# Gated mix of a state-space scan and a GELU layer: skip seeded into PSUM, gate as a weight column, B scale folded into C, shorter sine tables, halved weight strips

## The chip, the cores and the metric

The kernel runs on one core of one Trainium2 chip. The metric is device microseconds of one execution. A profile's span runs from the first to the last instruction; in these runs an execution is 1.8 to 2.1 us longer than its span. The granted TensorE clock of a run is its mean share of full speed; it was 0.99 to 1.00, and it is named where it matters.

Engines: PE is TensorE's matmul stream, PEld its weight loads, DVE is VectorE, ACT is ScalarE, POOL is GpSimd, SP issues most DMAs. A name with a q (SPq) is an engine's sequencer. PSUM is the memory into which TensorE writes; the program uses it as eight banks. An evacuation is the operation that reads a finished bank and so frees it. A hole is idle time of PE within a stage.

## The reference

One input x of 2048 x 640 goes through two branches, mixed by a gate per row:

```
g   = sigmoid(sum(x * gate_w))                       # per row
a   = 2 * Re(C @ h) + x * Dskip,  h_t = Lam_bar * h_(t-1) + B_bar @ x_t   # complex, 640 states
      with Lam_bar = exp(dt * Lam),  B_bar = ((Lam_bar - 1) / Lam) * (B_re + i B_im)
b   = gelu(x @ w1 + b1) @ w2 + b2                    # 640 -> 1728 -> 640
out = g * a + (1 - g) * b                            # bfloat16
```

## The kernel before

Rows are handled in 4 chunks of 512 (`CH`); the code counts them from 0, the text and the tables from 1. Per chunk PE does four stages: `ff1` (x·w1), `ssm` (B·x), `fin_b` (·w2) and `fin_a` (C·h). VectorE does the recurrence: it rotates B·x by a table of cosines and sines, so that the complex recurrence becomes two real scans, and rotates back. The rotation back carries the factor 2(Lam_bar - 1)/Lam in two tables of its own (OCOS, OSIN).

PE, VectorE and ScalarE execute in the order in which the program emits instructions. The author chooses VectorE's order at build time with an assumed clock: pending scan pieces are let out until the time at which an urgent operation is expected to be ready.

```python
    class Clock:
        pe = 6.5; act = 13.0; dve = 0.0
    def let_out(until):                      # emit pending scan pieces that would start before `until`
        while pend:
            ready, cost, fn = pend[0]
            start = max(ck.dve, ready)
            if start >= until: return
            pend.pop(0); fn(); ck.dve = start + cost
    def dve_now(ready, cost, fn):            # an urgent operation: after the pieces that fit before it
        let_out(ready); fn(); ck.dve = max(ck.dve, ready) + cost
    ...
    def ff1(c, group):                       # ff1(0, 7), later chunks ff1(c, 1)
        for g0 in range(0, KF, group):       # KF = 14 tiles of 128 columns of w1, the last of 64
            kfs = range(g0, min(KF, g0 + group))
            for kd in range(KD):             # KD = 5 strips of w1
                for kf in kfs:               # one PSUM bank per kf: `group` banks at once
                    if kd == 0: banks[kf] = bank()
                    ff1_mm(banks[kf], sizes[kf], c, kf, kd)
            ...                              # then the GELUs (ACT), from PSUM to SBUF
    ff1(0, 7)
    ...                                      # sine tables TCOS, TSIN, OCOS, OSIN, diag on VectorE
    ck.dve = 30.0                            # from here the scans are assumed to start
    ...
    def gates():                             # 80 matmuls with one column each
        for ti in range(NT):
            for kd in range(KD):
                nc.tensor.matmul(p[:, ti:ti + 1], lhsT=xT[c][:, kd, lo:lo + P], rhs=gw_c[:, kd:kd + 1], ...)
    def fin_a(c):
        for a in range(TPC):                 # 4 row tiles of 128
            for d0, d1 in cuts(ti):          # 384 + 256 columns
                p = bank()
                for j in range(2 * KS):
                    nc.tensor.matmul(p[:, 0:d1 - d0], lhsT=hs[c][:, j, lo:lo + P], rhs=CT[:, j % KS, d0:d1],
                                     start=(j == 0), stop=False)
                for o in range(d0, d1, P):   # skip term: x times a diagonal matrix
                    nc.tensor.matmul(p[:, o - d0:o - d0 + P], lhsT=xT[c][:, kd, lo:lo + P], rhs=diag[:, kd, :], ...)
                def f():                     # evacuation: ot = g * p + gb, frees the bank
                    nc.vector.scalar_tensor_tensor(out=ot[:, d0:d1], in0=p[:, 0:d1 - d0], scalar=gcol[:, 0, ti:ti + 1], ...)
                dve_now(ck.pe + 0.2, 0.5, f)
    ssm(0); ff1(1, 1); ssm(1); gates(); fin_b(0); fin_a(0)
    ssm(2); ff1(2, 1); fin_b(1); fin_a(1)
    ssm(3); ff1(3, 1); fin_b(2); fin_a(2); fin_b(3); fin_a(3)
```

## Time and profile before

The median was 235.54 us (235.34 to 235.76, four runs). The profiled run had a span of 234.1 us; the spans of other runs were mostly 233.0 to 233.9, so this profile is a slightly slow specimen.

Lines of the page of the kernel before follow: busy time of each engine with its share of the span and its instruction count; of part 2 the rows of PE and DVE over 40 equal slices (tenths busy); and of part 4 the chain of waits by engine.

```profile
PE 223.4 (95%) x1425; PEld 130.0 (56%) x1438; DVE 187.4 (80%) x429; ACT 87.6 (37%) x148; POOL 5.5 (2%) x16
...
PE   7978999999999999889999999999999999999994
...
DVE  1899999999999999999999999999999913300132
...
PE 65%; DVE 27%; issue 2%; ACT 2%; DMA 1%; ACTq 0%; DVEq 0%
```

PE is busy 95%, VectorE 80%, and the row of VectorE shows 9 from about 12 to 187 us: it has hardly a free moment there. The waits view of PE (who waited for whom; total us, times, longest):

```profile
PE bank L255 <- ACT gel L260: 2.4, 6, 1.4
PE bank L407 <- DVE ot L475: 2.2, 4, 0.9
```

The second line: B·x (L407) needs PSUM banks that the evacuation of C·h (ot, L475) has not yet freed. On PE's timeline (start, length, line, operation, idle before it and who ended it) the first line's hole looks like this:

```profile
15.71 0.38 PE L255 MATMUL bank<-xT_76,w_0_80 128*128 128x512 bf16 x1
17.49 0.38 PE L255 MATMUL bank<-xT_76,w_0_80 128*128 128x512 bf16 x1 [1.40 <-ACT gel L260]
18.07 0.38 PE L255 MATMUL bank<-xT_76,w_0_80 128*128 128x512 bf16 x1 [0.20 <-ACT gel L260]
...
27.63 0.39 PE L407 MATMUL bank<-xT_76,BT_re 128*128 128x512 bf16 x1
```

From 15.7 us PE gets one bank per GELU (0.58 us) instead of one per 0.216 us. ACT's timeline says why it began so late:

```profile
14.93 0.51 ACT L233 ACTIVATE hs<-gel,halfpi 128x256 f32<-128x256 f32 x1
15.45 1.28 ACT L260 ACT_TABLE_LOAD   x1
16.75 1.84 ACT L260 ACTIVATE gel<-bank,colB 128x512 bf16<-128x512 f32 x3
```

The gate matmuls and one cut of C·h on PE's timeline:

```profile
64.55 0.64 PE L422 MATMUL bank<-gw_c,xT_76 128*128 128x1 bf16 x20
...
66.56 1.62 PE L448 MATMUL bank<-w_sb,gel 128*128 128x384 bf16 x9
...
81.81 0.98 PE L465 MATMUL bank<-CT_re,hs 128*128 128x384 bf16 x5
82.62 0.98 PE L465 MATMUL bank<-CT_im,hs 128*128 128x384 bf16 x5
83.43 0.33 PE L470 MATMUL bank<-diag,xT_76 128*128 128x128 bf16 x3
83.60 0.71 PE L465 MATMUL bank<-CT_re,hs 128*128 128x256 bf16 x5
```

Three diagonal matmuls occupy PE from 83.43 to 83.60, although the groups view states 219 ns for one. Start-to-start is what counts, not stated durations: matmuls overlap. Last, VectorE's first scan piece, and the late evacuation of the first C tile, whose first cut PE had left at 83.60 us:

```profile
42.94 0.90 DVE L338 TENSOR_SCALAR diag<-ident,colB 128x128 bf16<-128x128 bf16 x5
43.76 0.68 DVE L347 TENSOR_TENSOR wa<-TCOS,bu 128x1024 bf16<-128x1024 bf16 x1
...
92.96 0.61 DVE L475 SCALAR_TENSOR_TENSOR ot<-bank,gcol,gb 128x384 bf16<-128x384 f32 x1
93.49 0.68 DVE L347 TENSOR_TENSOR wb<-TSIN,bu 128x1024 bf16<-128x1024 bf16 x1
94.09 0.48 DVE L475 SCALAR_TENSOR_TENSOR ot<-bank,gcol,gb 128x256 bf16<-128x256 f32 x1
```

### The profile page before, as it was taken

To read this page: it belongs to the slowest core of one execution; us is meant where nothing else is said; L and a number is where in the kernel's file an instruction comes from. 1 tells how busy PE (TensorE), PEld (TensorE's weight loads), DVE (VectorE), ACT (ScalarE), POOL (GpSimd) and SP (SyncE) were. 2 spreads that over 40 slices of the span, in tenths; PEclk is the share of its full clock that TensorE was granted. 3 is DMA by queue.
4 is the path that set the end of the run, shared out by engine and by line. 5 is a ranking of instruction groups with operands and counts; after the bars stand their busy time and mean duration, and the time that the engine had idled before them with its cause. 6 is when DMAs were issued, how large, how long until landed. Compare 5 with 4: busy or idle time off the path is not lost.

```text
span 234.1 us, 3628 instructions
## 1 busy us (share of the span) xinstructions
PE 223.4 (95%) x1425; PEld 130.0 (56%) x1438; DVE 187.4 (80%) x429; ACT 87.6 (37%) x148; POOL 5.5 (2%) x16
## 2 busy tenths in 40 slices
PE   7978999999999999889999999999999999999994
PEld 3532344444486777334446777644446767776672
DVE  1899999999999999999999999999999913300132
ACT  2885575655510500345662310146563220022100
POOL 6000000000000000000000000000000000000000
PEclk9999999999999999999999999999999999999999
DMA  6999899400000000110000000020000000100011
GB/s 186 327 224 198 212 335 195 96 3 0 1 3 0 3 0 0 56 59 0 0 1 3 0 0 3 28 84 0 3 0 0 0 3 28 60 28 0 3 56 56
DMA packets 26352, 13.18 MB, mean 56 GB/s; under 512 B 21407, under 2 KB 25696, under 8 KB 26336
## 3 DMA queue, kind: packets, MB, share of 16 engines
q1 hardware_dynamic: 26178, 12.95, 22.1%
q8 instruction: 11, 0.18, 0.3%
q14 instruction: 5, 0.04, 0.1%
q0 software_dynamic: 128, 0.01, 0.0%
q10 hardware_dynamic: 30, 0.00, 0.0%
HBM read 5.09 MB, written 2.62 MB: 33 GB/s over the span
## 4 chain that ended last, share of the span: by engine, by line
PE 65%; DVE 27%; issue 2%; ACT 2%; DMA 1%; ACTq 0%; DVEq 0%
PE bank L448 20%; PE bank L255 16%; PE bank L465 14%; PE bank L407 13%; DVE g L366 7%; DVE wb L347 4%; DVE wa L347 4%; DVE ot L475 3%; DVE hs L347 2%; DVE v L347 2%; ACT gel L260 2%; PE bank L470 1%; DMA prmA<-in_A_Lambda_re_dram 1%; DVE gel L230 1%; PE bank L199 1%
## 5 line engine op out<-in xcount | busy, mean ns | idle before, releaser
L448 PE MATMUL bank<-w_sb,gel 128*128 128x384 bf16 (+3 forms) x447 | 61.6, 299 | 0.1
L448 PEld LDWEIGHTS <-gel 128*128 128x128 bf16 x448 | 43.0, 98 | 18.6 <-issue 0.8
L260 ACT ACTIVATE gel<-bank,colB 128x512 bf16<-128x512 f32 (+1 forms) x56 | 37.1, 689 | 22.5 <-PE bank L255 22.5
L475 DVE SCALAR_TENSOR_TENSOR ot<-bank,gcol,gb 128x384 bf16<-128x384 f32 (+3 forms) x32 | 16.9, 545 | 34.5 <-PE bank L470 29.1
L410 ACT ACTIVATE bu<-bank 128x512 bf16<-128x512 f32 x40 | 23.6, 597 | 44.7 <-PE bank L407 43.1
L451 ACT ACTIVATE gb<-bank,gcol 128x384 f32<-128x384 f32 (+3 forms) x32 | 16.4, 529 | 56.5 <-PE bank L448 47.4
L366 DVE TENSOR_TENSOR_SCAN g<-r_c,carry,v 128x512 bf16<-128x512 f32 x30 | 37.0, 1271 | 0.0
L465 PEld LDWEIGHTS <-hs 128*128 128x128 bf16 x320 | 29.8, 98 | 10.2
L465 PE MATMUL bank<-CT_re,hs 128*128 128x384 bf16 (+3 forms) x159 | 26.9, 299 | 0.1
L465 PE MATMUL bank<-CT_im,hs 128*128 128x384 bf16 (+3 forms) x160 | 27.0, 299 | 0.0
L407 PEld LDWEIGHTS <-BT_re 128*128 128x128 bf16 x100 | 9.5, 98 | 14.0 <-issue 3.5
L407 PEld LDWEIGHTS <-BT_im 128*128 128x128 bf16 x100 | 9.8, 98 | 12.2 <-issue 0.5
L347 DVE TENSOR_TENSOR v<-wa,wb 128x512 bf16<-128x512 bf16 x40 | 15.2, 422 | 0.7
L347 DVE TENSOR_TENSOR wa<-OCOS,g 128x1024 bf16<-128x1024 bf16 x20 | 13.7, 687 | 0.2
L347 DVE TENSOR_TENSOR wb<-TSIN,bu 128x1024 bf16<-128x1024 bf16 x20 | 13.7, 685 | 0.0
L347 DVE TENSOR_TENSOR wa<-TCOS,bu 128x1024 bf16<-128x1024 bf16 x20 | 13.7, 684 | 0.0
L347 DVE TENSOR_TENSOR wb<-OSIN,g 128x1024 bf16<-128x1024 bf16 x20 | 13.7, 684 | 0.0
L255 PEld LDWEIGHTS <-w_0_80 128*128 128x128 bf16 (+1 forms) x56 | 5.4, 98 | 11.3 <-issue 5.2
L366 DVE TENSOR_TENSOR_SCAN g<-r_c,v 128x512 bf16<-128x512 f32 x10 | 11.7, 1209 | 0.0
L255 PEld LDWEIGHTS <-w_3_83 128*128 128x128 bf16 (+1 forms) x56 | 5.4, 99 | 6.9 <-issue 0.7
L255 PEld LDWEIGHTS <-w_4_84 128*128 128x128 bf16 (+1 forms) x56 | 5.4, 99 | 6.9 <-issue 0.7
L255 PEld LDWEIGHTS <-w_1_81 128*128 128x128 bf16 (+1 forms) x56 | 5.4, 99 | 6.8 <-issue 0.9
(144 smaller groups left out, 268.6 us busy)
## 6 DMA issues: line engine op xcount, KB each, us to landing
out_dram<-ot SPq DMA_DIRECT2D x15, 160.0 KB, 1.8
w_sb<-in_B_w_dram SPq DMA_DIRECT2D x1, 2080.0 KB, 8.7
hs<-in_A_x_dram SPq DMA_DIRECT2D x2, 320.0 KB, 3.3
w_0_80<-in_B_w_dram SPq DMA_DIRECT2D x1, 432.0 KB, 6.1
w_1_81<-in_B_w_dram SPq DMA_DIRECT2D x1, 432.0 KB, 6.7
w_2_82<-in_B_w_dram SPq DMA_DIRECT2D x1, 432.0 KB, 7.4
w_3_83<-in_B_w_dram SPq DMA_DIRECT2D x1, 432.0 KB
w_4_84<-in_B_w_dram SPq DMA_DIRECT2D x1, 432.0 KB, 8.2
```

Source lines behind the costliest of these rows:

```text
L199: nc.tensor.transpose(pT[:, a * P:(a + 1) * P], x0n[a // H][:, a % H, kd * P:(kd + 1) * P], ident[:])
L230: nc.vector.scalar_tensor_tensor(out=red[:, ks, :], in0=tf[:], scalar=thp_c[:, ks:ks + 1], in1=kk[:], op0=ALU.mult, op1=ALU.subtract)
L255: nc.tensor.matmul(p[:m, :], lhsT=w1_sb[kd][:, kf * P:kf * P + m], rhs=xT[c][:, kd, :], start=(kd == 0), stop=(kd == KD - 1))
L260: nc.scalar.activation(out=gel[c][:m, kf, :], in_=p[:m, :], func=ACT.Gelu_apprx_tanh, bias=b1_c[:m, kf:kf + 1])
L347: nc.vector.tensor_tensor(out=o, in0=a, in1=b, op=op)
L366: nc.vector.tensor_tensor_scan(s["g"][:, ri, :], r_c[:, ks:ks + 1].to_broadcast([P, CH]), s["v"][:, ri, :], init, ALU.mult, ALU.add)
L407: nc.tensor.matmul(p[:], lhsT=BT[:, kd, ks * P:(ks + 1) * P], rhs=xT[c][:, kd, :], start=(kd == 0), stop=(kd == KD - 1))
L410: nc.scalar.activation(out=bu[:, ri, :], in_=p[:], func=ACT.Identity)
L448: nc.tensor.matmul(p[:, 0:d1 - d0], lhsT=gel[c][:m, kf, lo:lo + P], rhs=w2_sb[:m, kf, d0:d1], start=(kf == 0), stop=(kf == KF - 1))
L451: nc.scalar.activation(out=gb[:, d0:d1], in_=p[:, 0:d1 - d0], func=ACT.Identity, scale=gcol[:, 1, ti:ti + 1])
L465: nc.tensor.matmul(p[:, 0:d1 - d0], lhsT=hs[c][:, j, lo:lo + P], rhs=CT[:, j % KS, d0:d1], start=(j == 0), stop=False)
L475: nc.vector.scalar_tensor_tensor(out=ot[:, d0:d1], in0=p[:, 0:d1 - d0], scalar=gcol[:, 0, ti:ti + 1], in1=gbs[ti][:, d0:d1], op0=ALU.mult, ...
```

## The change

The intent is to take work off PE: the skip term is written into the PSUM bank by VectorE before the C matmuls, which then only accumulate (`start=False`); the gate is a 65th output row of the last w1 tile. To make room on VectorE, the factor (Lam_bar - 1)/Lam is folded into C once (20 operations of 640 columns, half of them on ACT) so that OCOS and OSIN vanish, and sines are computed for a quarter of a chunk in two wide ACT operations and extended by rotation. Each w1 strip is loaded in two halves, and after the first seven tiles of the first chunk the others are taken one at a time.

```diff
-    w1_sb = [const.tile([P, F], BF16, name=f"w1_{kd}") for kd in range(KD)]
+    w1a = [const.tile([P, cut1], BF16, name=f"w1a_{kd}") for kd in range(KD)]     # cut1 = 7 tiles
+    w1b = [const.tile([P, n1b], BF16, name=f"w1b_{kd}") for kd in range(KD)]      # last column: gate_w
 ...
-            kfs = range(g0, min(KF, g0 + group))
+        groups = [range(0, FA)] if c == 0 else []
+        groups += [[kf] for kf in range(FA if c == 0 else 0, KF)]
 ...
+        if kf == KF - 1:      # row 64 of the last tile is the gate
+            nc.scalar.activation(out=zrow[F_LAST:F_LAST + 1, :], in_=p[F_LAST:F_LAST + 1, :], func=ACT.Tanh, scale=0.5)
+            ...               # four small DMAs turn the row into columns gz
 ...                           # OCOS, OSIN, diag and gates() removed
-    ck.dve = 30.0
+    ck.dve = 27.0
 ...
+    def fold(ks):             # CT_re, CT_im scaled in place: ACT makes t1, t2, VectorE combines
+        ...
+        dve_now(ready, 0.8, lambda: f(CT_re, c2re, t1))
+        dve_now(ready, 0.8, lambda: f(CT_im, n2re, t2))
 ...
+    def seed(ti):
+        for d0, d1 in cuts(ti):                      # 320 + 320 columns
+            p = bank()
+            dve_now(ck.pe, 0.45, lambda: nc.vector.tensor_tensor(out=p[:, 0:d1 - d0], in0=xn[c][:, a, d0:d1], in1=Dbc[:, d0:d1], op=ALU.mult))
 ...
     def fin_b(c):
+            if a == TPC - 1:
+                seed(c * TPC)
     def fin_a(c):
-                p = bank()
+            if a < TPC - 1:
+                seed(ti + 1)                         # one tile ahead
+                p = seeded[ti][i]
-                                     start=(j == 0), stop=False)
-                for o in range(d0, d1, P):
-                    ...                              # diagonal matmuls
+                                     start=False, stop=(j == 2 * KS - 1), skip_group_check=True)
```

Carry arithmetic of the scans is batched over the five state tiles as well, and the warm-up has seven matmuls instead of eight.

## The prediction

> **What bounds the kernel now.** TensorE. The page shows PE busy 95% of the 234.1 us span at full granted clock; PE's timeline is back-to-back stages: first dense chunk from 7.92 to 27.63 us (19.7), then per chunk 10.8 for B·x, 15.3 for the first dense layer, 15.25 for the second, 11.98 for C·h with the skip. Start-to-start is 216 ns for 512 columns, 163 for 384, 109 for 256, which agrees with the Trainium skill, "TensorE: Matmul & The Clock Gate", section on 56 against 53.3 ns (columns over 2.4 GHz plus about 2.5 ns). So PE time is columns; cutting 640 as 320+320 instead of 384+256 gains nothing.
>
> VectorE is 80% busy, without a gap from 14 to 187 us, but rarely holds PE: the waits view gives 2.2 us of PE waiting for the output evacuation (PSUM banks), all in the third and fourth chunk's B·x, and 2.4 us for GELU evacuation in the first chunk.
>
> **Removed from PE, all on the critical path**
> - Skip by diagonal matmuls: a C stage falls from 11.98 to 10.87 us, 1.1 x 4 = 4.5 us.
> - Gate matmuls: 64.55 to 66.56 us = 2.0 us (25 ns each, far less than their durations suggest). The gate column rides in the last dense tile, free.
> - First dense chunk: 70 x 0.216 = 15.1 us of work takes 19.7. PE stood near 16 to 17.5 us, then went in steps of 0.58 us, because seven banks were requested at once while ACT was still at its sines (last one 14.93, table load 15.45, first GELU 16.75). Now the sines are two wide operations, so the GELU table is loaded by about 13 us, and the second seven tiles come one at a time: about 4.2 us.
> - Half strips: the first strip landed at 7.9 us; half of it saves about 0.6; start near 7.3.
> - Bank waits: VectorE started its scans at 43.8 us where the schedule assumed 30, so evacuations were ordered late. The tables now end near 29 us against an assumed 27: about 1.8 of the 2.2 us.
>
> Sum 13.1 us.
>
> **Added, mostly off the path.** VectorE: 33 seeds (estimate 0.42 us each; the skill, "VectorE: DVE Perf Modes", tier table, has tensor_tensor at 1x with any PSUM operand; the 256-column evacuation took 0.39 us to the next), ten folds (about 0.8 us), six wide rotations (4.7). It loses the OCOS/OSIN tables (15.7 us, 27.25 to 42.94), most carry arithmetic (0.54 x 15), half the phases. Net about -3 us, busy near 184, but 14 us earlier at the start. ACT gains about 10 us, at 37% busy. New PE waits: seeds in the first two C stages (1.7 us of seeds and evacuation per 2.7 us tile, plus scans of 1.2 us), and folds before the first C stage (about 3 us of slack). I allow 1.5 us.
>
> **Prediction.** 235.55 - 13.1 + 1.5 = 224, shaded to 223.0 us because the stage sum (7.3 + 15.4 + 193.6 + 3.4 tail + 1.45 outside the span) gives 221. Range 220.5 to 227. Faster by over 2%: 0.96; same: 0.03; slower: 0.01.
>
> **Right if:** no gate or diagonal matmuls, about 150 fewer; first dense chunk about 15.5 us, ending near 23; C stages 10.9; scans beginning near 29 us; PE busy about 210 us; waits for seeds under 2 us.
>
> **Wrong if:** VectorE is late on seeds or folds (PE stops at C stages; several us); gate DMAs land late behind the loads, blocking VectorE in order; transposed B arrives after 23 us now that ten strips precede it.

## The result, and the profile after

The median was 220.99 us (220.52 to 221.08, four runs), 0.938 of before (95% interval 0.936 to 0.939): 14.5 us less, and 2.0 us below the predicted 223.0; that is inside its range, 0.5 us above the lower end. Ratios are the mean time of one kernel's fast runs over that of the other's of the same rounds, so not quite the ratio of the medians quoted.

Lines of the page of the kernel after that answer to those of before:

```profile
PE 213.4 (97%) x1276; PEld 125.1 (57%) x1287; DVE 189.3 (86%) x393; ACT 94.6 (43%) x153; POOL 5.0 (2%) x15
...
PE   7999999999999999999999999999999999999994
...
DVE  1979999999999999999999999999999999800173
...
DVE 74%; PE 19%; issue 3%; DMA 2%; SPq 0%; DVEq 0%
```

VectorE did not get lighter: 189.3 us against 187.4. Its row is at 9 from about 16 to 186 us. PE's waits (the wait of 1.2 us before its very first instruction, in both kernels, is left out):

```profile
PE bank L508 <- DVE bank L475: 0.7, 2, 0.5
PE bank L278 <- DMA w1a_80<-in_B_w_dram: 0.3, 1, 0.3
```

The hole in the first dense chunk is gone; PE goes on at 0.216 us a matmul:

```profile
12.46 1.68 PE L278 MATMUL bank<-xT_76,w1a_84 128*128 128x512 bf16 x7
13.98 0.38 PE L278 MATMUL bank<-xT_76,w1b_85 128*128 128x512 bf16 x1
14.19 0.38 PE L278 MATMUL bank<-xT_76,w1b_86 128*128 128x512 bf16 x1
```

ACT's timeline shortly before:

```profile
12.82 1.28 ACT L283 ACT_TABLE_LOAD   x1 [1.39 <-DVE colB L306]
14.12 1.26 ACT L283 ACTIVATE gel<-bank,colB 128x512 bf16<-128x512 f32 x2
```

The first GELU came at 14.12 us: the table load waited for the biases (colB), not for the sines, which were done at 11.4. C·h has no diagonal matmuls:

```profile
73.47 0.84 PE L508 MATMUL bank<-CT_re,hs 128*128 128x320 bf16 x5
74.15 0.84 PE L508 MATMUL bank<-CT_im,hs 128*128 128x320 bf16 x5
74.83 0.84 PE L508 MATMUL bank<-CT_re,hs 128*128 128x320 bf16 x5
```

VectorE begins its scans 15.7 us earlier:

```profile
28.09 0.69 DVE L379 TENSOR_TENSOR wa<-TCOS,bu 128x1024 bf16<-128x1024 bf16 x1
```

The new wait, first on PE's timeline:

```profile
180.32 0.84 PE L508 MATMUL bank<-CT_im,hs 128*128 128x320 bf16 x5
181.66 0.84 PE L508 MATMUL bank<-CT_re,hs 128*128 128x320 bf16 x5 [0.50 <-DVE bank L475]
```

At the same time on VectorE, two seeds (L475) stand behind a scan (L398):

```profile
179.80 1.28 DVE L398 TENSOR_TENSOR_SCAN g<-r_c,carry,v 128x512 bf16<-128x512 f32 x1
...
181.12 0.90 DVE L475 TENSOR_TENSOR bank<-xn,Dbc 128x320 f32<-128x320 bf16 x2
```

PE's last row before the wait starts at 180.32 and five matmuls take 0.68 us, so the next should have begun at 181.00; it began at 181.66. The waits view counts only 0.50 of these 0.66 us, because it begins where the modelled end of the pipelined matmul lies. So stages are best compared by their starts. This table is worked out from one profile of each kernel, from PE's timelines, each stage from its first matmul's start to that of the next stage's; the last column belongs to an experiment below. The start varies from profile to profile: 6.88 to 7.92 us in the seven with whole strips, 6.17 to 6.53 in the seven with halves.

| PE stage, us | before | after | seeds two tiles ahead |
|---|---|---|---|
| start of the first dense matmul | 7.92 | 6.20 | 6.17 |
| first dense layer, chunk 1 | 19.71 | 15.33 | 15.34 |
| the same, each later chunk | 15.32 | 15.11 | 15.11 |
| B·x, chunks 1 and 2 | 10.80 | 10.79 | 10.79 |
| gates | 2.01 | none | none |
| B·x, chunk 3 | 13.06 | 10.79 | 10.79 |
| B·x, chunk 4 | 11.40 | 10.79 | 10.79 |
| second dense layer, each | 15.25 | 15.25 | 15.25 |
| C·h, chunks 1, 2, 3 | 11.98 each | 11.21, 11.31, 11.71 | 10.87, 10.86, 10.87 |
| C·h, chunk 4 | 12.15 | 11.05 | 11.06 |
| from the last matmul's end to the span's end | 3.28 | 2.90 | 2.89 |

The chain of waits changed its face, from PE 65% and DVE 27% to DVE 74% and PE 19% (the last lines of the two pages above). Read naively this says that VectorE now bounds the kernel. The experiments test that.

### The profile page after: what moved, and what is told of

Its sections match the earlier page's. It is cut to its first block, busy times and chain, and to the rows that moved or that the text cites. A ratio compares the mean times of both kernels' runs of the same rounds, so it can differ in the third digit from the quotient of the medians.

```text
span 219.2 us, 3326 instructions
## 1 busy us (share of the span) xinstructions
PE 213.4 (97%) x1276; PEld 125.1 (57%) x1287; DVE 189.3 (86%) x393; ACT 94.6 (43%) x153; POOL 5.0 (2%) x15
## 4 chain that ended last, share of the span: by engine, by line
DVE 74%; PE 19%; issue 3%; DMA 2%; SPq 0%; DVEq 0%
DVE g L398 19%; DVE wb L379 11%; DVE wa L379 10%; PE bank L508 9%; PE bank L489 7%; DVE v L379 7%; DVE hs L379 6%; DVE ot L513 3%; DVE bank L475 3%; PE bank L278 3%; DMA w1a_80<-in_B_w_dram 2%; DVE CT_re L367 2%; DVE CT_im L367 2%; DVE g L329 1%; DVE TSIN L330 1%
## 5 line engine op out<-in xcount | busy, mean ns | idle before, releaser
L489 PE MATMUL bank<-w_sb,gel 128*128 128x320 bf16 x448 | 61.6, 299 | 0.0
L398 DVE TENSOR_TENSOR_SCAN g<-r_c,carry,v 128x512 bf16<-128x512 f32 x30 | 37.1, 1269 | 0.0
L492 ACT ACTIVATE gb<-bank,gcol 128x320 f32<-128x320 f32 x32 | 16.4, 528 | 46.2 <-PE bank L489 46.2
L508 PE MATMUL bank<-CT_re,hs 128*128 128x320 bf16 (+2 forms) x165 | 27.1, 295 | 0.8 <-DVE bank L475 0.7
L513 DVE SCALAR_TENSOR_TENSOR ot<-bank,gcol,gb 128x320 bf16<-128x320 f32 (+2 forms) x33 | 17.6, 534 | 11.9 <-PE bank L508 11.7
L508 PE MATMUL bank<-CT_im,hs 128*128 128x320 bf16 (+2 forms) x165 | 27.1, 295 | 0.0
L475 DVE TENSOR_TENSOR bank<-xn,Dbc 128x320 f32<-128x320 bf16 (+2 forms) x33 | 14.4, 481 | 6.3 <-ACT gb L492 6.3
L379 DVE TENSOR_TENSOR wa<-TCOS,g 128x1024 bf16<-128x1024 bf16 x20 | 13.7, 685 | 0.1
L379 DVE TENSOR_TENSOR wb<-TSIN,g 128x1024 bf16<-128x1024 bf16 x20 | 13.7, 683 | 0.0
L398 DVE TENSOR_TENSOR_SCAN g<-r_c,v 128x512 bf16<-128x512 f32 x10 | 11.7, 1208 | 0.0
L379 DVE TENSOR_TENSOR hs<-wa,wb 128x512 bf16<-128x512 bf16 x20 | 8.5, 423 | 0.6
L379 DVE TENSOR_TENSOR hs<-wb,wa 128x512 bf16<-128x512 bf16 x20 | 8.4, 418 | 0.0
```

What stands on the lines that cost most here:

```text
L379: nc.vector.tensor_tensor(out=o, in0=a, in1=b, op=op)
L398: nc.vector.tensor_tensor_scan(s["g"][:, ri, :], r_c[:, ks:ks + 1].to_broadcast([P, CH]), s["v"][:, ri, :], init, ALU.mult, ALU.add)
L475: dve_now(ck.pe, 0.45, lambda: nc.vector.tensor_tensor(out=p[:, 0:d1 - d0], in0=xn[c][:, a, d0:d1], in1=Dbc[:, d0:d1], op=ALU.mult))
L489: nc.tensor.matmul(p[:, 0:d1 - d0], lhsT=gel[c][:m, kf, lo:lo + P], rhs=w2_sb[:m, kf, d0:d1], start=(kf == 0), stop=(kf == KF - 1))
L492: nc.scalar.activation(out=gb[:, d0:d1], in_=p[:, 0:d1 - d0], func=ACT.Identity, scale=gcol[:, 1, ti:ti + 1])
```

## The experiments

Two kernels were the base: before (names b_) and after (names a_). Each run was timed beside runs of the kernel before on the same chip, whose medians were 235.34, 235.30 and 235.49 us in the three sessions. The kernel after itself was timed once, in a session of its own, at 220.99, so differences of medians from it are between sessions. Taken from the ratios to before of the same rounds instead, they are -1.3 us for a_noseed, 0.0 for a_nofold, +1.9 for a_group7, +1.7 for a_fullstrip, -1.5 for a_lead2, -1.3 for a_ck28 and +1.7 for a_ck13.

### b_ck41: only VectorE's order

```diff
-    ck.dve = 30.0
+    ck.dve = 41.0
```

> The kernel before, with one number of its build-time schedule changed: VectorE is assumed to begin its scans at 41 us instead of 30 (they began at 43.8). No instruction is added or removed, only VectorE's order changes. Theory (evacuations were placed late in VectorE's order because the schedule was wrong by 14 us): the bank waits in the third and fourth B.x stages, 13.06 and about 11.4 us against 10.8 undisturbed, go away, -2.0 to -2.7 us. Rival (VectorE is simply too loaded, and only removing work frees the banks): within 0.5 us of before.

Measured 234.03 us, ratio 0.992 (0.989 to 0.996). In its profile PE has no wait for VectorE's evacuations left, and both B·x stages take 10.79 us. So it is the order and not the amount of work that held the banks. Yet the time fell by only 1.3 us at the median. The four runs suggest why: 232.38 us at a granted clock of 0.998, and 233.99, 234.07 and 234.10 at 0.991. The lower clock cost this kernel 1.7 us, whereas before ran 235.13 to 235.97 at 1.00 and 235.13 to 235.75 at 0.993. At the better clock the gain is about 3 us, but that is a single run; the stages of its profile agree (2.88 us less in the two B·x stages). At the median the expected 2.0 to 2.7 was missed.

### b_m65: 65 rows instead of 64

```diff
-    w1_sb = [const.tile([P, F], BF16, ...)]
+    w1_sb = [const.tile([P, F + 1], BF16, ...)]      # last column set to zero
 ...                                                  # five memsets on VectorE for it, and the loads' slices, left out
-        nc.tensor.matmul(p[:m, :], lhsT=w1_sb[kd][:, kf * P:kf * P + m], ...)
+        mm = m if m == P else m + 1
+        nc.tensor.matmul(p[:mm, :], lhsT=w1_sb[kd][:, kf * P:kf * P + mm], ...)
```

> The kernel before, with its last dense tile given 65 output rows instead of 64 (a zero column of weights; the result is unchanged). Theory, formed from the two traces: around the ten-matmul-or-fewer group of 64 rows there are two holes of about 0.1 us per chunk, absent at 65 rows; the dense stage falls from 15.32 to 15.11 us, -0.8 us over four chunks. Rival (the 0.2 us came from something else, such as the ends of the stages): 0.

Measured 235.48 us, ratio 1.000 (0.999 to 1.002): nothing. But the stage did what the theory said: 15.11 us instead of 15.32 in chunks 2 to 4. In before, the hole is seen where the 64-row tile starts and where it ends; 0.31 us lie between starts instead of 0.216:

```profile
52.24 0.38 PE L255 MATMUL bank<-xT_77,w_4_84 128*128 128x512 bf16 x1
52.55 0.40 PE L255 MATMUL bank<-xT_77,w_0_80 128*64 128x512 bf16 x1
...
53.44 0.38 PE L255 MATMUL bank<-xT_77,w_4_84 128*64 128x512 bf16 x1
53.75 0.82 PE L407 MATMUL bank<-xT_77,BT_re 128*128 128x512 bf16 x3
```

The Trainium skill, "TensorEngine Tiling (Array Packing)", Key Properties, says that changing the tiling mode drains TensorE; 128x64 is in the page's list under Available Configurations. The trace agrees, with about 0.1 us at each change. That the drain is the reason, and not something else that 64 rows bring, was not separated. Where did the 0.8 us go? Chunk 3's B·x took 13.22 us instead of 13.06 and chunk 4's 11.61 instead of 11.40. Part was visibly returned at the bank wait; the next experiment shows how.

### b_singles: seven banks at once, or one tile at a time

```diff
-        for g0 in range(0, KF, group):
-            kfs = range(g0, min(KF, g0 + group))
+        groups = [range(0, 7)] + [[kf] for kf in range(7, KF)] if c == 0 else [[kf] for kf in range(KF)]
+        for kfs in groups:
+            g0 = kfs[0]
```

> The kernel before, with the second seven tiles of the first dense chunk taken one at a time (five matmuls into one bank) instead of seven banks at once; the sines stay as late as they were. Theory (the hole of 4.4 us is mostly that seven banks are asked for at once): one tile runs while ACT loads its table, PE waits about 0.7 us, then follows; -3.2 to -3.7 us. Rival (the late sines alone make the hole): nearly nothing, since the first GELU still starts at 16.75 us.

Measured 235.90 us, ratio 1.002 (1.000 to 1.005). Here again the stage obeyed: the first dense chunk took 15.78 us (7.79 to 23.57) instead of 19.71, with the sines as late as ever. PE was 4 us ahead, and lost it all again. VectorE's instructions are in the same order in both traces. PE's waits in this experiment:

```profile
PE bank L408 <- DVE ot L476: 5.4, 5, 3.1
```

(L408 and L476 are here B·x and the evacuation.) The longest of these waits on PE's timeline:

```profile
89.62 0.28 PE L471 MATMUL bank<-diag,xT 128*128 128x128 bf16 x2
92.99 1.24 PE L408 MATMUL bank<-xT,BT_re 128*128 128x512 bf16 x4 [3.09 <-DVE ot L476]
```

PE finished the first C·h at 89.9 us and stood 3.09 us for a bank that VectorE had not evacuated, because in VectorE's order that evacuation lay behind scans which themselves started at 43.1 us (43.8 in before). The third B·x ended at 106.85 us in before, at 106.26 in b_m65 and at 106.20 here. PE came to that stage at 93.79 and 93.04, and here would have come at 89.74 (its C·h stage started at 77.75 and takes 11.99 undisturbed). The end followed VectorE: its scans started at 43.76, 43.19 and 43.13, so the 0.6 us by which the stage ended earlier are VectorE's own, and PE's 0.8 and 4 us brought nothing. That point was pinned by VectorE, and PE's 95% hid it. It would also explain why before did not feel the lower clock: in b_m65's profile, at 0.993, the clock is below full only from 16 to 24 us (0.80 and 0.78 in its two halves), long before the pinned stage.

### b_ck41_singles: both

The two edits above together; the result is correct.

> The kernel before with both edits that did little alone: the schedule's start of the scans at 41 us (-1.3 us alone) and the second seven tiles one at a time (+0.5 us alone). Theory (each saving of PE time before the third B.x stage was returned there because late evacuations held the banks; with the order mended nothing holds it): first dense chunk about 15.7 us, perhaps 0.6 us of waiting for the first scan results, together -4 to -5.3 us, near 230.5. Rival (the two simply add): -0.8 us.

Measured 229.07 us, ratio 0.975 (0.971 to 0.978): -6.4 us, where the two alone sum to -0.8. The sum mixes clocks, since three of four runs of b_ck41 had the lower one. Like with like, each against its session's median of before: at 0.998 to 1.00 the two alone give -3.0 (one run) and +0.4, together -6.4; at 0.991 to 0.993 they give -1.3 and +1.4 (one run), together -4.5 (one run). Either way the two together gain some 4 us more than their sum. PE waits for no evacuation, the first C stage takes 11.99 us, and the first dense chunk 15.86. One of its four runs, at clock 0.993, took 231.03, the others 228.94 to 229.08. It went beyond the expected -5.3; no wait of PE for the first scan results is in its waits view.

### b_nodiag: the skip term dropped

The loop of diagonal matmuls is removed (the result is wrong).

> The kernel before without the 80 diagonal matmuls: the skip term is missing, so the result is wrong on purpose. Theory (a 128-column matmul costs its start-to-start of 56 ns): -4.4 us, C stages 10.87 instead of 11.98, plus or minus 0.4 from shifted bank waits. Rival (it costs its stated duration of 219 ns): up to -9.6 us, the union of their busy time.

Measured 231.90 us, ratio 0.985 (0.983 to 0.987): -3.4 us. C stages took 10.87 and 10.86 us instead of 11.98, so the 1.11 us a stage are right and the 219 ns stated are not the cost. The time fell by less than 4.4 us: in the profile, at clock 0.993, the first dense chunk took 20.61 us instead of 19.71, and the bank waits of both B·x stages moved (11.53 and 12.23 us instead of 13.06 and 11.40). The edit also takes the diagonal matmuls out of the assumed clock, so that VectorE's evacuations stand elsewhere in its order; it does not change PE's work alone.

### a_noseed: no seeds

Seeds removed and `start=(j == 0)` restored (skip term missing, wrong).

> The changed kernel without its 33 seeds (skip term missing, result wrong on purpose; PE's matmuls unchanged). Theory (stage lengths: the first three C stages are 11.21, 11.31 and 11.71 us against 10.87): PE's waits for seeds go, -1.6 us, to about 219.4. Rival A (what the waits view says, 0.7 us): 220.3. Rival B (the chain of waits, 74% VectorE, means that VectorE bounds the kernel): 13 us of VectorE work less brings many us.

Measured 219.41 us, ratio 0.932 (0.931 to 0.934), 1.6 us below the kernel after. The first three C stages are 10.87 us. So the seeds' waits cost 1.6 us (1.3 by the ratios) and not the 0.7 of the waits view. VectorE's busy time fell from 189.3 to 177.1 us, and that brought nothing beyond it.

### a_nofold: no folds

`fold(ks)` is not called (C unscaled, wrong): 8.8 us of stated durations less on VectorE and 8.2 on ACT; their busy times fell from 189.3 to 182.3 us and from 94.6 to 87.5.

> The changed kernel without the ten folds on VectorE and the ten on ACT (C not scaled, result wrong on purpose). PE's work is unchanged. Theory (PE bounds; VectorE's order leaves waits only at the seeds): within 0.6 us of the changed kernel. Rival (VectorE's chain bounds, as 74% in the chain of waits suggests): 8 us of VectorE work less, several us faster.

Measured 220.71 us, ratio 0.938 (0.936 to 0.939), 0.3 us below after. The rival falls: the 74% in the chain of waits is not a bound. The chain steps to VectorE at a wait of a few tenths of a us (the 0.50 at 181.66 above), and from there finds VectorE almost always busy, back to about 14 us. The C stages took 11.60, 11.26 and 10.87 us here, so 1.1 us of waits for seeds remain, none of them in the waits view.

### a_group7: seven banks at once again

```diff
-        groups += [[kf] for kf in range(FA if c == 0 else 0, KF)]
+        groups += [range(FA, KF)] if c == 0 else [[kf] for kf in range(KF)]
```

> The changed kernel, with the second seven tiles of the first dense chunk again asking for seven banks at once; the sines stay early. Theory: ACT starts evacuating near 12.9 us at 0.58 us each while PE asks for a bank each 0.216 us from 14.0, so PE loses about 1.1 us (0.8 to 1.5). Rival (the whole 4.4 us hole belongs to the grouping): +3 to +4 us.

Measured 222.52 us, ratio 0.946 (0.944 to 0.947): +1.5 us. The stage itself lost 2.5 us (17.81 instead of 15.33), more than expected, since I had ACT begin at 12.9 us and it begins at 14.1. One us came back: with PE later, and VectorE's order a little changed with it, the waits for seeds shrank (C stages 10.87, 10.94, 11.40).

### a_fullstrip: whole strips

Five loads of 432 KB instead of ten halves.

> The changed kernel with whole weight strips (five loads of 432 KB instead of ten of about 220). Theory: the first dense matmul waits for the first strip, 6.2 us now and 7.9 before; +1.3 to +1.8 us. My prediction had put the half strips at 0.6 us; rival, that the other changes at the start (seven warm-up matmuls, transposes by halves) made the rest: +0.6 us.

Measured 222.64 us (221.99 to 224.65), ratio 0.945 (0.943 to 0.948): +1.65 us. The first dense matmul starts at 7.91 us against 6.20; the idle time before it is a wait for its strip:

```profile
7.91 7.90 PE L276 MATMUL bank<-xT,w1f 128*128 128x512 bf16 x28 [1.74 <-DMA w1f<-in_B_w_dram]
```

The profile is of the slowest of the four runs: its clock fell to 0.58 between 8 and 12 us, after this start, and its first dense chunk took 17.02 us instead of 15.33. The times of the other three, 221.99 to 223.14, are 1.0 to 2.2 above the kernel after. So the halves make the earlier start in the main. How exactly, the spread of the starts under whole strips (6.88 to 7.92 us) leaves open.

### a_lead2: seeds two tiles ahead

```diff
             if a == TPC - 1:
                 seed(c * TPC)
+                seed(c * TPC + 1)
 ...
-            if a < TPC - 1:
-                seed(ti + 1)
+            if a < TPC - 2:
+                seed(ti + 2)
```

> The changed kernel with every seed placed two tiles ahead of its C matmuls instead of one (same instructions, result correct). Theory (the seeds are only late by up to a scan's length, because VectorE runs a little behind the schedule; there are banks for it): the C stages become 10.87 us and PE's waits for seeds vanish as they did without seeds, -1.3 to -1.7 us, near 219.4. Rival (PSUM banks run short: two current, four seeded, two being evacuated): PE waits elsewhere instead, no gain or slower.

Measured 219.46 us (219.02 to 219.71), ratio 0.932 (0.930 to 0.933), correct. It beats both kernels, by 1.5 us the kernel after, whose interval (0.936 to 0.939) lies clear of it. C stages as in the table's last column; the waits of PE are a single line, its very first instruction:

```profile
PE bank L191 <- DVE halfpi L186: 1.2, 1, 1.2
```

It runs as fast as the kernel without any seed (219.41): 33 operations on a VectorE that is 87% busy are now free. Its chain of waits, with the same instructions as the kernel after, is PE again:

```profile
PE 98%; DVE 1%; issue 0%
```

### a_ck28: the schedule's numbers corrected

```diff
-    ck.dve = 27.0
+    ck.dve = 28.2
-        later(0, 0.1 if ks < KS - 1 else 0.5, f5)
+        later(0, 0.1 if ks < KS - 1 else 0.65, f5)
-                later(0, 1.6, factors)
+                later(0, 2.35, factors)
```

> The changed kernel with its schedule's three assumed numbers set to what the trace shows (scans begin at 28.2 us instead of 27.0, the factors take 2.35 instead of 1.6, the last carry 0.65 instead of 0.5); same instructions in a slightly other order. Theory (the seeds are late because VectorE runs 1 to 2 us behind the schedule): part of the 1.6 us of waits goes, -0.4 to -1.2 us. Rival (the waits come from a scan of 1.2 us that happens to be ahead of a seed, whatever the offset): within 0.3 us, either sign.

Measured 219.69 us, ratio 0.933 (0.931 to 0.934), correct: -1.3 us, at the strong end of what I expected. All seed waits are gone (C stages 10.86 to 10.87). So the waits came from the order that the assumed clock had chosen; this fits VectorE running 1 to 2 us behind that clock, of which three numbers were changed at once. Either cure suffices; the two were not run together.

### a_ck13: the schedule made wrong

```diff
-    ck.dve = 27.0
+    ck.dve = 13.0
```

> The changed kernel with its schedule made wrong by the 14 us by which the schedule of before was wrong (scans assumed from 13 us). VectorE's work is the same, seeds and evacuations come later in its order. Theory (VectorE's order decides, and seeds made PE depend on it directly): the first C stage waits for seeds behind some 14 us of scans; +7 to +14 us. Rival (14 us of lateness cost before only 2 to 3 us, so here too): +2 to +4 us.

Measured 222.57 us, ratio 0.945 (0.944 to 0.946): +1.6 us. Both expectations were too high. The first C stage takes 12.38 us instead of 11.21 and the second dense layer before it 15.63 instead of 15.25; the others hardly change. The likely reason, argued and not tested: a scan piece enters VectorE's order only once its B·x is expected, so that the assumed lead shrinks whenever VectorE runs out of expected work. In this profile only one piece of the second chunk stands before the folds. In before VectorE was truly late, by 15.7 us more of tables.

## Why the prediction was right

The range held, and the kernel's stages fell as described, but the sum was made of parts of mixed quality:

| Term | predicted, us | measured from the stages, us |
|---|---|---|
| diagonal matmuls | 4.5 | 4.4 (3 x 1.11 + 1.10, from the last column) |
| gate matmuls | 2.0 | 2.01 |
| first dense chunk | 4.2 | 4.38, of which 0.2 from 65 rows |
| earlier start | 0.6 | 1.72 (7.71 - 6.40 = 1.3 by the medians of all profiles) |
| bank waits in B·x | 1.8 | 2.88 (13.06 + 11.40 - 2 x 10.79) |
| later dense chunks | not seen | 0.63 (3 x 0.21) |
| end of the span | 0 | 0.38 |
| waits for seeds and folds | +1.5 | +1.63 (11.21 + 11.31 + 11.71 - 2 x 10.87 - 10.86) |

- The mis-sized term is "the first strip landed at 7.9 us; half of it saves about 0.6". I took the strip's own transfer. With halves in the queue it saved 1.72 us in this pair of profiles and about 1.3 by the medians of all, at least double; a_fullstrip shows the strips to be the main cause. Why halving brings more than half a strip's share was not settled: the first 432 KB strip took 6.1 us from issue to landing and the first 224 KB strip 4.4.
- The bank waits were read from the waits view (2.2 us) instead of the stage lengths (2.88). The seeds' waits show the same bias, 0.7 against 1.6.
- The removed terms gave 224, and the prediction was shaded down to 223.0 because its sum of stages gave 221, which is what was measured. That the stage sum hit was luck: its start (7.3) and tail (3.4) were 1.1 and 0.5 us too long, its middle (193.6) was 1.2 too short against the measured 194.8 with the waits for seeds in it, and its time outside the span (1.45) 0.3 too short.
- "VectorE: net about -3 us, busy near 184" was wrong: 189.3, so +1.9. Seeds took 14.4 us, folds 8.8, rotations 4.9, all by stated durations. It did no harm: scans started 15.7 us earlier (28.1; predicted 29). No run separates this start from the order. An estimate says that both were needed: in b_ck41_singles, with the order mended but the scans still starting at 43.0, the first chunk's states were ready at 77.7 us, just in time for a C·h that starts at 77.60; in the kernel after it starts at 73.47, some 3 us or more too early for such scans.
- The first dense chunk was credited to the earlier sines and to the single tiles together. b_singles (15.78 us with late sines) against a_group7 (17.81 with early sines) shows that the single tiles do nearly all of it. Early sines without single tiles bring at most 1.9 (19.71 against 17.81), and on top of single tiles only some 0.2 to 0.3. The GELU table was loaded at 14.1 us, not 13, and for another reason.
- "All on the critical path" was wrong for the kernel before, as an argument. b_singles and b_m65 show that PE savings of 4 and 0.8 us alone were worth nothing there, since late evacuations pinned the third B·x. The terms added up only because the same change gave VectorE an order to match, and scans early enough for it. b_ck41_singles shows the part of the order with two edits: some 4 us more together than summed. The gate matmuls' 2.0 us is a stage length; no run removes them alone.
- PE busy was predicted near 210 us and is 213.4: holes that vanish were not busy time, so they cannot come off it. Matmul instructions fell by 149, as predicted.
- Of the dangers named, blocked gate DMAs and late B did not occur; late seeds did, at 1.6 us.
- The skill's spacing of matmuls ("TensorE: Matmul & The Clock Gate") held in every undisturbed stage: 15.11 us for 70 matmuls of 512 columns is 0.216 each. "VectorE: DVE Perf Modes", tier table, also held: two seeds of 320 columns took 0.80 us from start to the next start, 0.40 each, which is 320 elements at one per cycle of the 0.96 GHz that "Trainium Kernel Development and Optimization", NeuronCore Architecture, gives for VectorE (0.33 us) and a rest. A seed of 128 columns took 0.22, so 192 columns more cost 0.18 us, near the 0.20 of that rate.

## What to carry to other kernels

Before adding up savings on the busiest engine, ask which point of its timeline another engine pins: PE at 95% with 2.2 us of waits still returned 4 us of savings at one evacuation. In a kernel whose order is chosen from an assumed clock, compare that clock with the trace first; one number was worth 1.3 us alone in before (3 at the better clock) and 6.4 us with a second edit. Measure waits by the length of a stage against its undisturbed twin, and test a chain of waits by removing work from the engine that it names; and give a producer that fills PSUM ahead of PE one more tile of lead than seems needed.

## What the Trainium skill lacked or had wrong

- "TensorEngine Tiling (Array Packing)", Key Properties, says that a mode switch drains TensorE but gives no cost. Here each change between 128 and 64 rows added about 0.1 us (0.31 us between starts instead of 0.216), 0.2 us per chunk; with 65 rows the stage keeps 0.216 us throughout.
- "PSUM — Partial Sum Buffer", among the consequences under The four PSUM rules, says that the only seed value safe either way is 0, because a matmul without the first flag overwrites where an earlier one left its bit clear. Here 33 non-zero seeds gave correct results in every run that kept them and did not spoil the result elsewhere, which is consistent with the page's rule for columns that an earlier group has written (the bits themselves were not looked at). The page does not offer this as a way to seed, though it let 4.4 us of matmuls go.
- "Trainium Kernel Development and Optimization", Performance Expectations, rightly calls matmul busy time a bad metric. No page that I read draws the consequence for waits, which begin at such a modelled end: PE's waits for seeds were 0.7 us in the view and 1.6 us by stage lengths, 1.3 to 1.6 by a_noseed.
- No page that I read tells what halving the loads of a queue does to the first one: 6.1 us to landing at 432 KB, 4.4 us at 224 KB, and 1.3 to 1.7 us at the kernel's start.
